# K and V blocks of a decode-attention loop requested as two halves of 64 partitions from two queues

## The chip, the cores and the metric

The kernel runs on one core of one Trainium2 chip. The metric is the device time of one execution in microseconds (us), and the median of several executions is compared. Beside it stands one profiled execution, from which all views of the profile are taken.

## The reference, cut to what matters

One token `x` of 448 values goes through two branches. The first is attention with 16 query heads over 8 groups of a cache of 65,536 keys and values of 256 numbers each (bf16); two query heads share one group. The second is a small token mixer. A sigmoid gate mixes the two.

```python
def _A_ref(x, k_cache, v_cache, wq, wo):
    B, Sq, D = x.shape
    Hq, Dh = 16, 256
    Hkv = k_cache.shape[1]
    rep = Hq // Hkv
    q = (x @ wq).reshape(B, Sq, Hq, Dh).transpose(0, 2, 1, 3)
    k = jnp.repeat(k_cache, rep, axis=1)
    v = jnp.repeat(v_cache, rep, axis=1)
    scores = jnp.einsum("bhqd,bhkd->bhqk", q, k) * (Dh ** -0.5)
    p = _softmax(scores, axis=-1)
    o = jnp.einsum("bhqk,bhkd->bhqd", p, v)
    return o.transpose(0, 2, 1, 3).reshape(B, Sq, Hq * Dh) @ wo
...
return g * a + (1 - g) * b      # g: gate, a: attention, b: mixer
```

K and V together are 8 x 65,536 x 256 x 2 values of 2 bytes, 537 MB. Each of them is used once.

## The kernel before, in words

The cache is cut into 32 blocks of 16,384 positions (`BLK`), four for each group. A block of K or of V is 128 partitions x 128 positions x 256 numbers, so that each partition reads one contiguous row of 65,536 bytes: 8.389 MB in all.

A loop over `t` runs 15 times and does two blocks, `e` = 0 and 1, in four stages. In the first stage of a block VectorE transposes K in eight pieces (`transposes`, L407) and TensorE multiplies each with the queries (`scores`, L415). In the second stage come the softmax (`softmax`, L472 to L511: the maximum, the Exp on ScalarE at L503, the transposed weights), the products with V (`pv`, L435) and the running sum (`accumulate`, L516). The last two blocks are written out behind the loop, with loads cut in other ways (L127, L135, L161); the first K block is requested ahead of it (L132).

K has three buffers of half a block each (`slots`, 64 positions of every partition). A block with `e` = 0 lies in the first two and is transposed upper half first, a block with `e` = 1 lies in the last two, so the next K can be requested when half of the block at hand is transposed. V has one buffer (`vt`), so the next V can be requested when the last product with the block at hand is done.

All large loads are requested by SP, in the order of the program: V of this block (`load_v`, L135), K of the next (`load_k_whole`, L132), and for `e` = 0 a piece of the output weights (`load_wo_wide`, L144), 32 rows of 7,168 bytes that are placed 4 partitions apart. ScalarE requests only the small tables ahead of the loop. In the loop ScalarE does, in this order, two copies of the spread output weights (L564, when TensorE's `spread_wo`, L560, is done), one more copy (L567), the Exp and a small Exp for the rescaling (L507), and again the two Exps for `e` = 1.

`seq` keeps every engine's instructions in the order of the program. The loop's semaphores are reset in turn at the four stages' ends: an engine that enters a stage waits until its own work of two stages before is done, SP's transfers among it (these waits carry the line L602 of the loop).

Of the kernel before, what the change touches and what calls it, by code (L numbers as in the profile page):

```python
# [21 lines left out]
KP = VP // 2  # L22
# [11 lines left out]
def kernel(  # L34
# [15 lines left out]
    nc = tc.nc  # L50
# [12 lines left out]
    def seq(ins):  # L63
        e = ins.ins.engine
        if e in last:
            tc.add_manual_dep(
                ins.ins,
                last[e],
                mybir.DependencyInfo(
                    mybir.DependencyClass.NoSync, mybir.DependencyReason.DATA  # L70
                ),
                reason="program order",
            )
        last[e] = ins.ins.name
        return ins
# [9 lines left out]
    k_all = kvpool.tile([128, 3 * KP, DH], BF16, name="k_all")  # L85
    slots = [k_all[:, i * KP:(i + 1) * KP, :] for i in range(3)]
    vt = kvpool.tile([128, VP, DH], BF16, name="vt")
# [35 lines left out]
    def rows(name, n):  # L123
        return flat[name][bass.ds(n, 1)].rearrange("o p j d -> (o p) j d")
# [6 lines left out]
    def load_k_whole(n, slot):  # L131
        seq(nc.sync.dma_start(out=k_all[:, slot * KP:(slot + 2) * KP, :], in_=rows("k", n)))  # L132

    def load_v(n, j0=0, j1=VP):
        seq(nc.sync.dma_start(out=vt[:, j0:j1, :], in_=rows("v", n)[:, j0:j1, :]))  # L135

    def pairs(ap):
        return ap.rearrange("p (i j) d -> p i j d", i=2)
# [4 lines left out]
    def load_wo_wide(h):  # L143
        seq(nc.sync.dma_start(  # L144
            out=wo_in[0:128:WS],
            in_=A_wo.rearrange("(h q c) n -> h q c n", q=128 // WS, c=WC)[bass.ds(h, 1)].rearrange(
                "o q c n -> (o q) c n"
            ),
        ))
# [9 lines left out]
    def load_v_last(n):  # L159
# [8 lines left out]
        out=wq_t[:, :], in_=A_wq[DM:D, :].rearrange("r (h n) -> (r h) n", h=2)  # L168
    ))
    seq(nc.sync.dma_start(out=wq_m, in_=A_wq[0:DM, :].rearrange("(p k) n -> p k n", k=3)))  # L170
    for k, table in enumerate((
# [19 lines left out]
        out=val[:], in_=rowsel[:, :, :, 0:NI], op=ALU.add, axis=AXIS.XY  # L191
    ))
    fst = const.tile([128, 2, REP], FP32)
    for e in range(2):
        seq(nc.vector.tensor_reduce(
            out=fst[:, e, :], in_=rowsel[:, :, :, e:e + 1], op=ALU.add, axis=AXIS.XY
# [3 lines left out]
        out=par[:], in_=ident_f[:].rearrange("p (a r) -> p r a", r=REP), op=ALU.add, axis=AXIS.X  # L200
# [3 lines left out]
        out=nval[:], in0=val[:], scalar1=-scale, scalar2=None, op0=ALU.mult  # L204
# [7 lines left out]
        out=same[:], in_=val[:].unsqueeze(1).to_broadcast([128, 64, REP])  # L212
# [8 lines left out]
        out=sel[:],  # L221
        in_=ident.rearrange("p (w k) -> p w k", w=NW).unsqueeze(2).to_broadcast([128, NW, NQ, 32]),
# [7 lines left out]
        out=xrr[:], in_=xr[:, DM:D].unsqueeze(2).to_broadcast([1, D - DM, 2])  # L230
    ))
    x_col = hd_ps[:, 40:44]
    for k in range(3):
# [13 lines left out]
        out=xtm[:], in0=par[:], scalar1=x_col[:, 3:4], scalar2=None, op0=ALU.mult  # L247
# [19 lines left out]
        out=veps[:], in0=mv[:, 1:2], scalar1=1e-5, scalar2=None, op0=ALU.add  # L267
# [5 lines left out]
    for _ in range(2):  # L273
# [3 lines left out]
            out=ntmp[:], in0=ntmp[:], scalar1=-0.5, scalar2=1.5, op0=ALU.mult, op1=ALU.add  # L277
# [3 lines left out]
        out=h_bc, in0=xf, scalar1=mv[:, 0:1], scalar2=rstd[:, 0:1],  # L281
        op0=ALU.subtract, op1=ALU.mult,
    ))
    for b in range(NF):
        seq(nc.scalar.activation(
            out=gel[b], in_=h_bc, func=ACT.Gelu_apprx_tanh,
# [33 lines left out]
    for k in range(2):  # L320
        seq(nc.vector.tensor_copy(
            out=qq[:, :, :, k, :], in_=qq_ps.rearrange("p (w g r) -> p w g r", g=HKV, r=REP)
# [72 lines left out]
    def turn():  # L395
        seq(nc.vector.tensor_scalar(
            out=caps[:], in0=caps[:], scalar1=-1.0, scalar2=None, op0=ALU.mult
        ))
        seq(nc.vector.tensor_scalar(
            out=ends[:], in0=ends[:], scalar1=-1.0, scalar2=1.0, op0=ALU.mult, op1=ALU.add  # L400
        ))
# [21 lines left out]
    def score_block(e, pair, hooks={}, order=FORWARD):  # L423
        for k, i in enumerate(order):
            transposes(pair, i)
            scores(e, i, k == 0, k == NI - 1)
            if k in hooks:
                hooks[k]()
# [92 lines left out]
    def denominators():  # L521
        seq(nc.tensor.matmul(  # L522
            hd_ps[:, 460:461], lhsT=same[:].rearrange("p a r -> p (a r)"), rhs=lsum[:, 0:1],
            start=True, stop=True,
        ))
        seq(nc.vector.reciprocal(out=rden[:], in_=hd_ps[:, 460:461]))
        seq(nc.vector.tensor_scalar(
            out=esc[:], in0=fst[:], scalar1=rden[:, 0:1], scalar2=ends[:, 0:1],
            op0=ALU.mult, op1=ALU.mult,
        ))  # L530
# [13 lines left out]
    def head_end():  # L544
        collect(esc, True, True)
        for c in range(2):
            seq(nc.vector.tensor_copy(out=oT[:, c, :], in_=o_ps[c]))  # L547
        a_ps = hd_ps[0:1, 0:D]
        for r in range(REP):
            for c in range(2):  # L550
                seq(nc.tensor.matmul(  # L551
                    a_ps, lhsT=oT[:, c, r:r + 1], rhs=wo_sb[:, r, c, :],
                    start=(r == 0 and c == 0), stop=(r == REP - 1 and c == 1),
                ))
        seq(nc.vector.tensor_tensor(out=a_acc[:], in0=a_acc[:], in1=a_ps, op=ALU.add))  # L555

    def spread_wo(r):
        for c in range(2):
            for u in range(WS):
                seq(nc.tensor.matmul(  # L560
                    wo_ps[c], lhsT=steps[:, WS - u:WS - u + 128], rhs=wo_in[:, 2 * u + c, :],
                    start=(u == 0), stop=(u == WS - 1),
                ))
            seq(nc.scalar.copy(out=wo_sb[:, r, c, :], in_=wo_ps[c]))  # L564

    def older_wo():
        seq(nc.scalar.copy(out=wo_sb[:, 0], in_=wo_sb[:, 1]))  # L567
# [3 lines left out]
    def products(e):  # L571
        for ip in range(NI // 2):
            pv(e, ip)
            if ip == 0:
                tc.previous_stage_wait(mybir.EngineType.PE)
        accumulate(e)
# [19 lines left out]
    def early_signals(i):  # L596
        def both():
            tc.previous_stage_wait(mybir.EngineType.PE)
            tc.previous_stage_wait(mybir.EngineType.DVE)
        return {i: both}  # L600

    with tc.For_i(0, HQ - 1, 1, iteration_sync="staggered") as t:  # L602
        for e in range(2):
            if e:
                tc.stage_boundary()
            if e == 0:
                spread_wo(1)
                head_end()
                older_wo()
            tc.previous_stage_wait(mybir.EngineType.Activation)  # L610
            score_block(
                e, (e, e + 1), early_signals(0), FORWARD if e else UPPER_FIRST
            )
            load_v(2 * t + e)
            tc.stage_boundary()
            if e == 0:
                load_k_whole(2 * t + 1, 1)
                load_wo_wide(t)
                softmax(e, may_begin=True)
                tc.previous_stage_wait(mybir.EngineType.DVE)  # L620
                tc.previous_stage_wait(mybir.EngineType.Activation)
                products(e)
            else:
                load_k_whole(2 * t + 2, 0)
                softmax(e, pair=t + 1)
                tc.previous_stage_wait(mybir.EngineType.DVE)
                tc.previous_stage_wait(mybir.EngineType.Activation)
                denominators()
                turn()
                products(e)  # L630
# [6 lines left out]
    for n in (L - 1, L):  # L637
# [4 lines left out]
        if n == L - 1:  # L642
            load_v(n, 0, 48)
            load_k(L, 0, 2)
            load_k(L, 1, 1)
            load_v(n, 48, VP)
        else:
            load_v_last(L)
            load_wo(HQ - 1, 1)
        if n < L:  # L650
            softmax(n % 2)
        else:
            def rest_base():
# [9 lines left out]
                out=lsv[:], in0=val[:], scalar1=lsum[:, 0:1], scalar2=None, op0=ALU.mult  # L663
# [8 lines left out]
                out=rdv[:], in0=rdv[:], scalar1=gcol[:, 0:1], scalar2=None, op0=ALU.mult  # L672
# [6 lines left out]
    for c in range(2):  # L679
# [9 lines left out]
        out=oT[:], in0=o_last, in1=rdv[:].unsqueeze(1).to_broadcast([128, 2, REP]), op=ALU.mult  # L689
# [43 lines left out]
```

## Time and profile before

| what | value |
|---|---|
| median of 3 runs | 1264.24 us (1263.73 to 1264.41) |
| the profiled execution's own time | 1264.3 us |
| its span, first to last instruction | 1262.5 us |
| mean granted TensorE clock | 0.813 |
| busy: PE, DVE, ACT | 821.7, 711.4, 75.6 us |
| bytes read | 544.22 MB, 431 GB/s over the span |
| K requests in the loop and ahead of it, request to landing | 28.1 us (median) |
| V requests in the loop, request to landing | 27.1 us (median) |

The span lies between the first and the last instruction; what the device time has beyond it (1.8 us) lies around it. Busy time is the time in which an engine executed something. The time from request to landing includes the wait behind transfers that were requested earlier. A queue q1 in the profile is SP's, q10 ScalarE's.

### The profile page before, as it was taken

To read this page: it belongs to the slowest core of one execution; us is meant where nothing else is said; L and a number is where in the kernel's file an instruction comes from. 1 tells how busy PE (TensorE), PEld (TensorE's weight loads), DVE (VectorE), ACT (ScalarE), POOL (GpSimd) and SP (SyncE) were. 2 spreads that over 40 slices of the span, in tenths; PEclk is the share of its full clock that TensorE was granted. 3 is DMA by queue.
4 is the path that set the end of the run, shared out by engine and by line. 5 is a ranking of instruction groups with operands and counts; after the bars stand their busy time and mean duration, and the time that the engine had idled before them with its cause. 6 is when DMAs were issued, how large, how long until landed. Compare 5 with 4: busy or idle time off the path is not lost.

```text
span 1262.5 us, 12356 instructions
## 1 busy us (share of the span) xinstructions
PE 821.7 (65%) x4818; PEld 330.5 (26%) x4818; DVE 711.4 (56%) x755; ACT 75.6 (6%) x163; POOL 4.8 (0%) x9
## 2 busy tenths in 40 slices
PE   4757566575676756677565766658656586665668
PEld 2222222232222222222222322213222132222224
DVE  5665456664556644566444665446654456654575
ACT  4000000000000000000000000000000000000000
POOL 1000000000000000000000000000000000000000
PEclk8887789777888877878778887788877788877979
DMA  9999999999999999999999999999999999999998
GB/s 414 434 435 432 437 432 432 437 434 418 451 434 418 444 420 436 429 438 432 439 432 439 432 432 439 432 439 432 432 439 432 439 432 432 439 432 435 424 435 351
DMA packets 11478, 544.36 MB, mean 431 GB/s; under 512 B 1513, under 2 KB 1644, under 8 KB 2636
## 3 DMA queue, kind: packets, MB, share of 16 engines
q1 hardware_dynamic: 11378, 544.22, 99.6%
q8 instruction: 6, 0.10, 0.0%
q14 instruction: 4, 0.03, 0.0%
q10 hardware_dynamic: 90, 0.01, 0.0%
HBM read 544.22 MB, written 0.00 MB: 431 GB/s over the span
## 4 chain that ended last, share of the span: by engine, by line
DMA 69%; PE 13%; DVE 12%; issue 4%; SPq 0%; ACT 0%; DVEq 0%
DMA k_all<-in_A_k_cache_dram 67%; PE sc L415 12%; DVE kT L407 12%; DMA k_all<-in_A_v_cache_dram 2%; PE pv_last L560 0%; PE f L560 0%; PE hd_ps L551 0%; PE f L694 0%; ACT p_sb L503 0%; SPq L161 0%; DVE rmax L472 0%; SPq L132 0%; PE sm_ps L537 0%; PE hd_ps L537 0%; PE sm_ps L490 0%
## 5 line engine op out<-in xcount | busy, mean ns | idle before, releaser
L415 PE MATMUL sc<-kT,qz 128*128 128x512 bf16 x2048 | 546.5, 417 | 318.6 <-DVE kT L407 318.4
L407 DVE STREAM_TRANSPOSE kT<-k_all 128x2048 f32<-128x2048 f32 x256 | 570.9, 2283 | 207.6 <-DMA k_all<-in_A_k_cache_dram 157.3
L415 PEld LDWEIGHTS <-qz 128*128 128x128 bf16 x2048 | 211.5, 103 | 652.0 <-issue 472.6
L435 PE MATMUL pv_ps<-vt,pT 128*4 128x512 bf16 x1968 | 173.5, 529 | 27.3 <-DVE pT L510 27.3
L516 DVE SCALAR_TENSOR_TENSOR acc<-acc,al,pv_ps 128x512 f32<-128x512 f32 x31 | 23.2, 747 | 161.8 <-PE pv_ps L435 161.8
L435 PEld LDWEIGHTS <-pT 128*4 128x4 bf16 x2000 | 57.2, 109 | 130.8 <-issue 85.9
L503 ACT ACTIVATE p_sb<-sc,nb 128x512 bf16<-128x512 f32 x32 | 22.0, 687 | 1022.7 <-DVE nb L499 1022.7
L472 DVE TENSOR_REDUCE rmax<-sc 128x1 f32<-128x512 f32 x32 | 22.1, 692 | 63.7 <-PE sc L415 63.7
L510 DVE STREAM_TRANSPOSE pT<-p_sb 128x512 bf16<-128x512 bf16 x32 | 22.8, 711 | 27.1 <-ACT p_sb L503 27.1
L522 PE MATMUL hd_ps<-lsum,same 128*128 128x1 f32 x30 | 7.6, 321 | 28.8 <-DVE lsum L511 28.8
L490 PE MATMUL sm_ps<-mrun,ones_f 1*128 1x2 f32 x64 | 12.1, 257 | 21.2 <-DVE mrun L489 12.9
L476 PE MATMUL sm_ps<-ident_f,rmax 128*1 128x128 f32 x32 | 8.7, 270 | 24.5 <-DVE rmax L472 24.5
L560 PE MATMUL pv_last<-wo_in,steps 128*128 128x448 bf16 x64 | 15.6, 369 | 5.1 <-DVEq L602 4.3
L560 PEld LDWEIGHTS <-steps 128*128 128x128 bf16 x128 | 11.6, 100 | 22.2 <-issue 14.0
L490 PEld LDWEIGHTS sm_ps<-mrun,ones_f 1*128 1x128 f32 x64 | 9.4, 183 | 27.4 <-DVE mrun L489 16.3
L555 DVE TENSOR_TENSOR a_acc<-a_acc,hd_ps 1x448 f32<-1x448 f32 x15 | 9.1, 608 | 12.3 <-PE hd_ps L551 12.3
L564 ACT CAST wo_sb<-pv_last 128x448 bf16<-128x448 f32 x16 | 8.5, 532 | 123.7 <-PE pv_last L560 123.7
L551 PE MATMUL hd_ps<-wo_sb,oT 128*1 128x448 bf16 x60 | 15.8, 351 | 0.0
L560 PE MATMUL f<-wo_in,steps 128*128 128x448 bf16 x64 | 15.5, 367 | 0.0
L567 ACT COPY wo_sb<-wo_sb 128x896 bf16<-128x896 bf16 x15 | 14.1, 937 | 14.5 <-PE hd_ps L551 14.5
L522 PEld LDWEIGHTS hd_ps<-lsum,same 128*128 128x128 f32 x30 | 6.3, 261 | 30.1 <-DVE lsum L511 30.1
L547 DVE CAST oT<-hd_ps 128x2 bf16<-128x2 f32 x15 | 2.4, 160 | 20.3 <-PE hd_ps L537 20.3
(124 smaller groups left out, 194.9 us busy)
## 6 DMA issues: line engine op xcount, KB each, us to landing
k_all<-in_A_k_cache_dram SPq DMA_DIRECT2D x2, 4096.0 KB
vt<-in_A_v_cache_dram SPq DMA_DIRECT2D x1, 5120.0 KB
k_all<-in_A_v_cache_dram SPq DMA_DIRECT2D x1, 4096.0 KB
wo_in<-in_A_wo_dram SPq DMA_DIRECT2D x15, 224.0 KB, 27.9
vt<-in_A_wq_dram SPq DMA_DIRECT2D x1, 3072.0 KB
vt<-in_A_v_cache_dram SPq DMA_DIRECT2D x1, 3072.0 KB
k_all<-in_A_v_cache_dram SPq DMA_DIRECT2D x1, 2048.0 KB
k_all<-in_A_v_cache_dram SPq DMA_DIRECT2D x1, 1024.0 KB
```

What stands on the lines that cost most here:

```text
L407: seq(nc.vector.transpose(out=kT_tiles[i % 2][:].rearrange("p j w k c -> p (j w k c)").bitcast(FP32), in_=slots[pair[i // 4]][:, i % 4 * N ...
L415: seq(nc.tensor.matmul(sc_tiles[e][:, :], lhsT=qz[:, 2 * w + c, 2 * (NI - i):2 * (NI - i) + 128], rhs=kT_tiles[i % 2][:, :, w, :, c], star ...
L435: seq(nc.tensor.matmul(dst[32 * grp:32 * grp + 2 * REP, :, :], lhsT=pT[:, 32 * jj + 2 * REP * ip:32 * jj + 2 * REP * (ip + 1)], rhs=pairs( ...
L472: seq(nc.vector.tensor_reduce(out=rmax[:], in_=sc_ps[:, :], op=ALU.max, axis=AXIS.X))
L490: seq(nc.tensor.matmul(sm_ps[:, 128:128 + REP], lhsT=ones_f[0:1, :], rhs=mrun[0:1, :], start=True, stop=True))
L503: seq(nc.scalar.activation(out=p_sb[:, :], in_=sc_ps[:, :], func=ACT.Exp, scale=scale, bias=nb[:, 0:1], accum_out=den[:, 0:1],))
L510: seq(nc.vector.transpose(out=pT[:, :], in_=p_sb[:, :]))
L516: seq(nc.vector.scalar_tensor_tensor(out=acc[:], in0=acc[:], scalar=al_tiles[e][:, 0:1], in1=src[:, :, :], op0=ALU.mult, op1=ALU.add,))
L522: seq(nc.tensor.matmul(hd_ps[:, 460:461], lhsT=same[:].rearrange("p a r -> p (a r)"), rhs=lsum[:, 0:1], start=True, stop=True,))
L551: seq(nc.tensor.matmul(a_ps, lhsT=oT[:, c, r:r + 1], rhs=wo_sb[:, r, c, :], start=(r == 0 and c == 0), stop=(r == REP - 1 and c == 1),))
L560: seq(nc.tensor.matmul(wo_ps[c], lhsT=steps[:, WS - u:WS - u + 128], rhs=wo_in[:, 2 * u + c, :], start=(u == 0), stop=(u == WS - 1),))
L567: seq(nc.scalar.copy(out=wo_sb[:, 0], in_=wo_sb[:, 1]))
```

## The change

`load_k_both` and `load_v_both` request a block in two transfers: partitions 0 to 63 from SP's queue, and partitions 64 to 127 from ScalarE's. Each has 64 rows of 65,536 bytes. They take the place of `load_k_whole` and `load_v` in the loop; ahead of the loop and behind it the loads stay as they were. V's request now stands ahead of the block's scores in the program. On SP the order of the requests is unchanged. On ScalarE the V half of `e` = 0 comes ahead of the copies of L564, the V half of `e` = 1 behind the Exps of `e` = 0, and each K half ahead of the Exp of its block.

```diff
+    halves = ((slice(0, 64), nc.sync), (slice(64, 128), nc.scalar))
+
+    def load_k_both(n, slot):
+        for p, queue in halves:
+            seq(queue.dma_start(
+                out=k_all[p, slot * KP:(slot + 2) * KP, :], in_=rows("k", n)[p]
+            ))
+
+    def load_v_both(n):
+        for p, queue in halves:
+            seq(queue.dma_start(out=vt[p], in_=rows("v", n)[p]))
...
             if e:
                 tc.stage_boundary()
+            load_v_both(2 * t + e)
             if e == 0:
                 spread_wo(1)
                 head_end()
...
             score_block(
                 e, (e, e + 1), early_signals(0), FORWARD if e else UPPER_FIRST
             )
-            load_v(2 * t + e)
             tc.stage_boundary()
             if e == 0:
-                load_k_whole(2 * t + 1, 1)
+                load_k_both(2 * t + 1, 1)
                 load_wo_wide(t)
...
             else:
-                load_k_whole(2 * t + 2, 0)
+                load_k_both(2 * t + 2, 0)
                 softmax(e, pair=t + 1)
```

## The prediction

> **What bounds it now.** I read the page's transfer rows first, then its chain, then one turn of the loop by windows, critical chain, SP's waits and its timeline. The page's rows of the sixteen DMA engines and of their queues:
>
> ```profile
> DMA packets 11478, 544.36 MB, mean 431 GB/s; under 512 B 1513, under 2 KB 1644, under 8 KB 2636
> q1 hardware_dynamic: 11378, 544.22, 99.6%
> q10 hardware_dynamic: 90, 0.01, 0.0%
> ```
>
> Queue q1 is SP's. Its packets fill 99.6% of sixteen engines' span, so about 0.4% (5 us) of the span is free of traffic; the window 1250 to 1262.5 alone, at a DMA share of 0.60, holds all of that. q10 is ScalarE's and carries only the small tables of the start. The chain agrees:
>
> ```profile
> DMA 69%; PE 13%; DVE 12%; issue 4%; SPq 0%; ACT 0%; DVEq 0%
> ```
>
> Its PE and DVE shares are no slack to be won: transfers run under them too, as the windows of whole turns show (the columns end in clock, DMA share and GB/s):
>
> ```profile
> 182.00:260.00 78.00, 49.15 (x284) 19.75 (x282) 43.08 (x45) 3.92 (x9) 0.00 (x0) 0.82 1.00 433
> 260.00:338.00 78.00, 52.31 (x300) 21.52 (x297) 44.18 (x47) 4.99 (x11) 0.00 (x0) 0.82 1.00 433
> ```
>
> One block of K or V is 128 rows of 65,536 bytes, 8.389 MB. In the trace's packet records a row is one packet; each engine takes 8 rows of a block, one behind the other, and 7,486 of 7,808 rows take exactly 2.418 us. So a block takes 8 x 2.418 = 19.34 us, and sixteen engines move 433.7 GB/s, the rate of the windows. A turn has four blocks and 0.55 us of wo_in (two rows of 0.272 us per engine): 77.9 us, against 78.3 between SP's V requests at 102.95 and 181.27. SP's requests come well ahead of their turn:
>
> ```profile
> 181.27 0.34 SPq L135 DMA_DIRECT2D vt<-in_A_v_cache_dram  x1
> 198.61 0.33 SPq L132 DMA_DIRECT2D k_all<-in_A_k_cache_dram  x1
> 199.19 0.49 SPq L144 DMA_DIRECT2D wo_in<-in_A_wo_dram  x1
> 216.73 0.34 SPq L135 DMA_DIRECT2D vt<-in_A_v_cache_dram  x1
> ```
>
> K landed at 187.9 and 226.7 (the critical chain), so V has the engines from 187.9 to 187.9 + 19.34 = 207.2. The K request of 198.61 comes 8.6 us before that end, the V request of 216.73 10 us before 226.7. What times a request is a buffer coming free, and a stage's end:
>
> ```profile
> SPq L602 <- DMA vt<-in_A_v_cache_dram: 243.8, 30, 9.2
> SPq L132 <- DVE kT L407: 238.4, 30, 8.5
> SPq L135 <- PE pv_ps L435: 153.4, 29, 6.2
> ```
>
> None of these waits shows as an idle DMA engine. The bound is the rate of the rows, 2.418 us each.
>
> **The change, part by part.** The loop runs 15 times; 60 requests of 8.389 MB become 120 of 4.194 MB, half of them on ScalarE. Everything before and behind the loop stays.
>
> Issue on ScalarE: 60 x 0.34 us (SP's row) = 20 us of its sequencer, at nothing. The K half waits for the transposes of its stage; behind it stands the Exp L503, which waits for VectorE's nb in any case (1022.7 us over 32), and at 211.41 it started 12.8 us after SP's K request. The V half waits for the last P.V product (its end about 181.2); behind it stands the cast L564, which at 182.04 waited for TensorE's spread_wo, so 0.34 us plus the start of an issue just fits between. Were the cast 0.3 us late, K's landing at 187.9 would still cover it; without cover it is 15 x 0.3 = 4.5 us, at most 20. load_v moves ahead of score_block in the text, but SP runs nothing of score_block and its V request keeps the same waits: nothing.
>
> SP's stage waits now take in both halves' landings: at equal rates of the two rings, nothing. Bytes are the same. End marks: 16 more packets of 9 ns per block, one per engine, 60 x 0.009 = 0.5 us, and 0.5 us is below what a measurement of this kernel can tell from no change (about 0.2%, 2.5 us).
>
> What is left, and is everything, is how the engines run the rows. Two facts bear on it. First, an engine that has packets in both rings takes one from each in turn: in the packet records, from 4.4 us on, one 256-byte packet of q10 stands between two 24,576-byte rows of q1, on engine after engine, and none runs beside another. Second, a request of 64 rows puts 4 on each engine, as 128 rows put 8 and wo_in's 32 rows put 2. Both halves are asked for within a microsecond, so all sixteen engines write a row of partitions 0 to 63, then all a row of 64 to 127.
>
> No row of this trace shows sixteen engines inside one half of the partitions, so the cost is bounded. Upper end: a row load of 128 partitions has one engine on each eighth-row group of 8 partitions at 27.1 GB/s (65,536 / 2.418), and no row shows a group of 8 taking more. With twice the engines per group in the half being written, each row takes 4.836 us, a block 38.7, and 60 blocks cost 60 x 19.34 = 1160.6 us more. Lower end: wo_in has 32 rows only, and each still ran at its full rate, 7,168 bytes in 0.272 us, so the engine alone may be the limit and the cost nil; but its rows lie 4 partitions apart over all 128, and are a ninth as long. Below nothing: size against time (7,168 in 0.272, 65,536 in 2.418) leaves 8.4 ns of fixed time per row, and if a second ring hid that, 60 x 8 x 0.0084 = 4.0 us would be gained. I take a value near the upper end: the wide 128-row loads are the nearest in length, and in them each part of the partitions gets 1/16 of the rate and never more. The full factor 2 needs all engines in step. Around 66 us of the span their rows start within 1.37 us, thirteen of sixteen within 0.44 us; a mean pair is some 0.4 us apart, 17% of a row, in which each has its half to itself; a block lands with its last pair, which is nearly in step. I take the middle, 10% saved: 0.9 x 1160.6 = 1045 us.
>
> [...]
>
> Sum on the profiled execution: its time is 1264.3 us (span 1262.5 and 1.8 around it), 0.06 above the median of 1264.24. 1264.2 + 1045 = 2309 us. The last loads (L127, L135, L161) keep 128 rows and their 19.34 us per block.
>
> What is late next: K's landing, as now. With 38 us per transfer the requests (10.7 us behind a landing) come far ahead of the engines, so no wait on SP or ScalarE matters.
>
> **Rivals.**
>
> Out of step: the engines slide apart, so that one writes the lower half while its partner writes the upper. For: with the sixteen starts spread over 1.37 of 2.418 us, a pair at the two ends is 57% out of step already, and single rows of up to 2.97 us push engines about. Against: in the loop an engine that runs ahead waits for the next request, and all start it together. At 57% for all pairs the cost is 0.43 x 1160.6 = 499 us, 1763 in all; the case runs from 1320 to 1900.
>
> No shared limit (not slower): the engine itself is the limit and partitions take what comes. For: 7,486 rows at one time to the nanosecond, and wo_in's 27 GB/s in 32 rows. Against: only its rows' spread. It decides if a row of a half still takes 2.418 us. Then the same rows run in another order and the two halves of a block land together: 0 to +1.5 us, 1264 to 1266. It is also the case in which the change does nothing, or in which the hardware deals rows by partition, so that one half is eight engines' work. [...]
>
> Rings out of phase: rows stay at 2.418 us, but wo_in's two packets per engine sit in SP's ring alone, so ScalarE's ring gets ahead by up to two rows, and V's lower half lands behind rows of the next K. V is needed at 212.98 (P.V starts) and landed about 207.2: 5.7 us, 2.4 rows of cover. If a third row comes between, P.V and then the next V request slip; at 2.4 us per turn that is 15 x 2.4 = 36 us, 1300; the case runs from 1267 to 1320.
>
> Faster: the 8.4 ns per row hidden by the other ring, 1264.2 - 4.0 = 1260.2. It needs an engine that begins a row of one ring before the other's ends; against it, the q10 packets of the start stand one behind the other. The loop has no other time to give.
>
> **How the numbers follow.** In step, near factor 2: 0.55. Out of step: 0.18. No shared limit: 0.16. Rings out of phase: 0.06. Faster: 0.05. Slower by over 0.2%: 0.55 + 0.18 + 0.06 = 0.79; within 0.2%: 0.16; faster: 0.05. The predicted time is that of the first case, 2309, whose own range is 1900 to 2430 (55% of the upper end: 1264 + 638 = 1902; the whole of it and 5 us of late casts and marks: 1264 + 1161 + 5 = 2430). For 8 in 10 the range must hold the first two cases and reach to a third; the one at 1264 is the next, so it runs from 1262 to 2430.
>
> **What would show it.** Right: q1 and q10 with about half the bytes each (some 290 and 252 MB); DMA share still near 1.00 but about 225 to 245 GB/s in the loop's windows; K's requests landing after some 60 to 75 us instead of 28; VectorE's wait L407 for k_all up from 157.3 us by about a thousand; the sixteen engines' rows at 4 to 5 us. No shared limit: 433 GB/s, split evenly, rows at 2.418 us. Rings out of phase: rows at 2.418 us, but windows with a share under 1.00, and TensorE's L435 waiting for vt. Casts in the way: L564 starting behind an issue of ScalarE, and the next wo_sb product late. The prediction is wrong in its one large term if a row of a half does not take about twice as long.

## The result and the profile after

The changed kernel takes 2492.22 us (2487.4 to 2496.72, 4 runs) against 1264.16: a ratio of 1.9715 (95% interval 1.9677 to 1.9753). Here and below, runs that lie more than 1.5% above the fastest of their kernel are slow executions, and comparisons leave them out. The profiled execution took 2487.4 us, with a span of 2485.4. Lines of the loop's body stand 12 further down than before (the transposes are L419, the scores L427, P.V is L447, the loop L614).

The page of the changed kernel, its transfer rows:

```profile
DMA packets 12438, 544.36 MB, mean 219 GB/s; under 512 B 2474, under 2 KB 2605, under 8 KB 3597
q1 hardware_dynamic: 7538, 292.56, 52.2%
q10 hardware_dynamic: 4890, 251.67, 47.7%
```

The bytes are those of before. The two queues hold what the change puts on them, and together they fill 99.9% of the engines' span. So the engines are not idle: they are slow, at 219 GB/s against 431 before. The loop's windows say by how much (the last three columns are clock, DMA share and GB/s):

```profile
200.00:356.00 156.00, 50.19 (x284) 20.29 (x284) 43.64 (x44) 3.92 (x9) 0.00 (x0) 0.65 0.99 210
356.00:512.00 156.00, 50.09 (x284) 20.05 (x284) 43.51 (x44) 3.92 (x9) 0.00 (x0) 0.66 1.00 210
```

A turn that did 433 GB/s does 210, at the same share. TensorE's work per turn is the same (50 us), at a lower granted clock, 0.65 against 0.82; it waits for data either way. Who waits now, of the groups of waits (us in total, times, longest):

```profile
DVE kT L419 <- DMA k_all<-in_A_k_cache_dram: 934.7, 31, 33.9
PE pv_ps L447 <- DMA vt<-in_A_v_cache_dram: 473.2, 30, 25.3
```

VectorE's wait for K was 157.3 us. TensorE's wait for V is new. And SP's own waits and the requests' times to landing (in the page's part on DMA issues, the last number is the median in us):

```profile
SPq L614 <- DMA k_all<-in_A_k_cache_dram: 963.6, 29, 34.2
SPq L614 <- DMA vt<-in_A_v_cache_dram: 842.2, 30, 33.9
SPq L141 <- DVE kT L419: 119.6, 17, 8.4
```

```profile
k_all<-in_A_k_cache_dram SPq DMA_DIRECT2D x31, 65.5
vt<-in_A_v_cache_dram ACTq DMA_DIRECT2D x30, 46.1
vt<-in_A_v_cache_dram SPq DMA_DIRECT2D x30, 73.6
k_all<-in_A_k_cache_dram ACTq DMA_DIRECT2D x30, 47.1
```

SP's requests of V land 27 us behind ScalarE's, and V is complete only with the slower half. No run shows why. My guess is that wo_in's packets are in SP's ring alone (a ring is here what one engine runs of one queue's packets), so that ScalarE's ring runs ahead. The packet records of the trace give the size of the loss. They name no engine, but a packet that begins where another ends can be put on the same engine. Of 7,808 rows of 65,536 bytes 126 took about 2.42 us (the first block, which is still whole). Of the others, 5,050 took between 4.75 and 5 us (mean 4.879) and 2,623 more than 5 us (mean 5.087).

### The profile page after: what moved, and what is told of

Its sections match the earlier page's. It is cut to its first block, busy times and chain, and to the rows that moved or that the text cites. A ratio compares the mean times of both kernels' runs of the same rounds, so it can differ in the third digit from the quotient of the medians.

```text
span 2485.4 us, 12694 instructions
## 1 busy us (share of the span) xinstructions
PE 819.3 (33%) x4818; PEld 331.0 (13%) x4818; DVE 711.4 (29%) x755; ACT 75.6 (3%) x163; POOL 4.8 (0%) x9
## 3 DMA queue, kind: packets, MB, share of 16 engines
q1 hardware_dynamic: 7538, 292.56, 52.2%
q10 hardware_dynamic: 4890, 251.67, 47.7%
## 5 line engine op out<-in xcount | busy, mean ns | idle before, releaser
L427 PE MATMUL sc<-kT,qz 128*128 128x512 bf16 x2048 | 543.5, 415 | 1096.9 <-DVE kT L419 1096.6
L419 DVE STREAM_TRANSPOSE kT<-k_all 128x2048 f32<-128x2048 f32 x256 | 570.8, 2283 | 983.0 <-DMA k_all<-in_A_k_cache_dram 934.7
L427 PEld LDWEIGHTS <-qz 128*128 128x128 bf16 x2048 | 210.7, 103 | 1428.1 <-issue 1247.0
L447 PE MATMUL pv_ps<-vt,pT 128*4 128x512 bf16 x1968 | 173.6, 529 | 473.2 <-DMA vt<-in_A_v_cache_dram 473.2
L447 PEld LDWEIGHTS <-pT 128*4 128x4 bf16 x2000 | 59.0, 109 | 576.2 <-issue 532.7
L502 PEld LDWEIGHTS sm_ps<-mrun,ones_f 1*128 1x128 f32 x64 | 9.4, 182 | 27.4 <-DVE mrun L501 16.3
L341 DVE COPY qz<-qq 32x16 bf16 (+1 forms) x64 | 10.5, 163 | 1.4
```

Source lines behind the costliest of these rows:

```text
L419: seq(nc.vector.transpose(out=kT_tiles[i % 2][:].rearrange("p j w k c -> p (j w k c)").bitcast(FP32), in_=slots[pair[i // 4]][:, i % 4 * N ...
L427: seq(nc.tensor.matmul(sc_tiles[e][:, :], lhsT=qz[:, 2 * w + c, 2 * (NI - i):2 * (NI - i) + 128], rhs=kT_tiles[i % 2][:, :, w, :, c], star ...
L447: seq(nc.tensor.matmul(dst[32 * grp:32 * grp + 2 * REP, :, :], lhsT=pT[:, 32 * jj + 2 * REP * ip:32 * jj + 2 * REP * (ip + 1)], rhs=pairs( ...
L502: seq(nc.tensor.matmul(sm_ps[:, 128:128 + REP], lhsT=ones_f[0:1, :], rhs=mrun[0:1, :], start=True, stop=True))
```

## The experiments

Three theories were set against each other first. "Half": all engines write into one half of the partitions at a time, and a half takes no more than half of the rate. "Turns": an engine that changes queue after every row loses time. "Reads": the rows of the cache that are read together collide.

**One queue.** The same halves, both from SP.

```diff
-    halves = ((slice(0, 64), nc.sync), (slice(64, 128), nc.scalar))
+    halves = ((slice(0, 64), nc.sync), (slice(64, 128), nc.sync))
```

> The same halves of 64 neighbouring partitions, both requested from SP's queue, the lower one first. Theory 'half' (all sixteen engines write into one half of the partitions at a time, and a half takes only half of the rate): rows stay near 4.85 to 4.95 us, 2430 to 2500 us in all. Rival 'turns' (an engine that changes queue after every row loses a row's time): rows back at 2.42 us, 1264 to 1270. Rival 'reads' (the rows of the cache that are read together collide): the same rows are read together, 2430 to 2500.

2544.79 us, a ratio of 2.0149 (2.0109 to 2.0189). "Turns" falls: with one queue the loss is larger, not gone. The page:

```profile
DMA packets 12438, 544.37 MB, mean 215 GB/s; under 512 B 2473, under 2 KB 2604, under 8 KB 3596
q1 hardware_dynamic: 12338, 544.22, 99.9%
```

In its packet records the pattern is regular. Each engine has four rows of one half and then four of the other; a row that follows a row of the same half takes 5.12 to 5.14 us, and the first row after a change of half mostly 4.82 to 4.94. The two queues of the change switch halves at most rows: of the 7,651 rows that can be joined to the row before them on their engine, 4,871 follow a row of the other half and take 4.88 us on average, the other 2,780 take 5.07. So most of its rows are of the cheaper kind. The shorter rows are what it gains over one queue, 53 us.

**Every second partition.** Two queues, 64 rows per request from neighbouring rows of the cache, but they land in the even and the odd partitions.

```diff
-    halves = ((slice(0, 64), nc.sync), (slice(64, 128), nc.scalar))
+    halves = ((slice(0, 128, 2), slice(0, 64), nc.sync), (slice(1, 128, 2), slice(64, 128), nc.scalar))
...
-                out=k_all[p, slot * KP:(slot + 2) * KP, :], in_=rows("k", n)[p]
+                out=k_all[p, slot * KP:(slot + 2) * KP, :], in_=rows("k", n)[r]
...
-            seq(queue.dma_start(out=vt[p], in_=rows("v", n)[p]))
+            seq(queue.dma_start(out=vt[p], in_=rows("v", n)[r]))
```

> Two queues and 64 rows a request as in the change, and the same rows of the cache in each request, but they land in every second partition (even ones from SP, odd ones from ScalarE), so that each request covers the whole width. In blocks 0 and 30 keys then meet the values of other positions, since one of the two is loaded elsewhere; the work is the same. 'half': 1264 to 1275 us, rows of 2.42 us. 'turns': about 2490. 'reads': about 2490.

1355.09 us, a ratio of 1.0718 (1.07 to 1.0736). The rows are back: 7,364 of 7,808 take 2.42 to 2.6 us. Number of rows, queues and rows read are those of the change; only the partitions differ, and they take away 1137 of 1228 us. Of the 91 us that are left, 71 are engines without work. The queues fill all but 76 us of this kernel's span, and all but 5 of before's:

```profile
q1 hardware_dynamic: 7538, 292.56, 51.5%
q10 hardware_dynamic: 4890, 251.67, 42.9%
```

The other 20 us are in slower rows (up to 3.7 us); most of these are the first that an engine runs after a time without work. SP's waits and a window of a loop's stretch:

```profile
SPq L141 <- DVE kT L419: 458.7, 30, 17.3
```

```profile
200.00:356.00 156.00, 95.44 (x512) 37.38 (x515) 85.25 (x84) 5.85 (x15) 0.00 (x0) 0.78 0.94 400
```

The K request waits for all eight transposes of the block, not for four: with the transposes of K beginning at 662.9 it goes out at 682.16, 19.2 us later, where before it was 10.6. With 8.6 us of lead gone the engines run dry (share 0.94). That this wait takes in transposes of the other buffer is how the program's waits came out for strided partitions, no property of the chip.

**Every second row.** The halves of the change, but each reads every second row of the cache.

```diff
-    halves = ((slice(0, 64), nc.sync), (slice(64, 128), nc.scalar))
+    halves = ((slice(0, 64), slice(0, 128, 2), nc.sync), (slice(64, 128), slice(1, 128, 2), nc.scalar))
```

> The halves of the partitions as in the change, two queues, but each request reads every second row of the cache (even rows to the lower half, odd rows to the upper). In blocks 0 and 30 keys meet the values of other positions, as before. 'half': as the change, 2430 to 2500 us. 'turns': about 2490. 'reads': well below, near 1264 if the neighbouring rows were the whole cause.

2498.05 us, a ratio of 1.9785 (1.9728 to 1.9842): the interval overlaps that of the change. "Reads" falls.

**K on SP, V on ScalarE, both whole.**

```diff
     def load_k_both(n, slot):
...
+        load_k_whole(n, slot)
...
     def load_v_both(n):
...
+        seq(nc.scalar.dma_start(out=vt[:], in_=rows("v", n)))
```

> Whole blocks of 128 partitions, K from SP's queue and V from ScalarE's, V's request where the change has it. 'half': 1264 us within 3 (each engine has its own partitions). 'turns': the two queues hold rows together for some 9 us of every 19 us block, so 1700 to 1900 us. 'reads': 1264. It also prices the moved V request and its place on ScalarE: nothing expected.

1274.54 us, a ratio of 1.0077 (1.0054 to 1.01). Two queues and the moved V request together cost some 10 us. "Half" expected at most 3: a small effect is missing from it. The guess was that ScalarE's rows of V get in between K's last rows and so make K late. The next two runs test that.

**V alone, every second partition, from two queues and from one.** K is whole on SP. The comments name the two runs.

```diff
+    halves = ((slice(0, 128, 2), nc.sync), (slice(1, 128, 2), nc.scalar))   # v_every_second
+    halves = ((slice(0, 128, 2), nc.sync), (slice(1, 128, 2), nc.sync))     # v_every_second_one_queue
...
     def load_k_both(n, slot):
...
+        load_k_whole(n, slot)
...
             seq(queue.dma_start(out=vt[p], in_=rows("v", n)[p]))
```

> V in two requests of 64 rows from two queues, even partitions from SP and odd ones from ScalarE, each from its own row of the cache; K whole on SP, requested after four transposes again. 'half': rows of 2.42 us, 1264 to 1276 us (ScalarE's rows of V may pass the last rows of K as in the run with K and V on two queues, which took 1274.5). If the 91 us that every second partition cost for K and V together came of the requests themselves and not of K's later request, about 1310.

> V in two requests of 64 rows, even and odd partitions, but both on SP's queue behind K. If the 11 us that the same rows cost from two queues came of ScalarE's rows of V passing the last rows of K, they are gone: 1264 to 1266 us. If they came of two requests in place of one, or of V's place in the program: 1275 us.

From two queues 1275.39 us (ratio 1.0089, 1.007 to 1.0108), from one 1264.38 (ratio 1.0001, 0.9992 to 1.001). So splitting a block in two requests and asking for V earlier in the text cost nothing here, and the second queue costs 11 us. VectorE's wait for K, first from two queues and then from one:

```profile
DVE kT L416 <- DMA k_all<-in_A_k_cache_dram: 179.8, 22, 16.3
```

```profile
DVE kT L416 <- DMA k_all<-in_A_k_cache_dram: 155.2, 30, 7.7
```

With one queue the longest wait for K is 7.7 us, with two 16.3. The reading that fits is that V's rows in a ring of their own run between K's, which were asked for first, and K is what the next block waits for. That rows of two queues mix on an engine, the changed kernel's records show (4,871 of 7,651 follow one of the other queue). The 80 us between 1355 and 1275 go with K's halves, whose late request is described above; no run shows that alone.

**V alone in the halves of the change.** K is whole on SP, `halves` as in the change.

```diff
     def load_k_both(n, slot):
-        for p, queue in halves:
...
+        load_k_whole(n, slot)
```

> Only V comes in the two halves, K stays whole on SP. If each half row costs by itself ('half'), half of the loss is left: 1264 + 1228 / 2 = 1878 us, in a range of 1850 to 1910. If the loss came of K and V halves standing in the way of each other, much less than half is left: below 1700.

2002 us (2001.73 and 2002.29; two further executions took 2055.63 and 2062.38): a miss for "half" as stated, since 738 of 1228 us are left, not 614. The rows account for 693 us of it. Rows of V's half that follow one another take 5.13 us. Where the two rings alternate, V's take 4.5 to 4.95, and K's whole-width rows between them 2.6 to 3.0 in place of 2.42. A row of V and the K row behind it together take some 7.5 us, as 5.13 and 2.42 do. So it reads as if a row of V handed part of its cost to the next row. Some 33 us more are engines without work: the queues fill all but 38 us of this kernel's span, and all but 5 of before's.

```profile
q1 hardware_dynamic: 9458, 418.39, 68.6%
q10 hardware_dynamic: 2490, 125.84, 29.5%
```

The last 11 us or so are in smaller packets that took longer; wo_in's, at 0.45 us against 0.27, are about half of it.

**Where the border lies.** Two kernels move the cut by 32 partitions, one from two queues and one from SP alone; a third cuts in four. The comments name the first two.

```diff
+    halves = ((slice(32, 96), nc.sync), (slice(0, 32), nc.scalar), (slice(96, 128), nc.scalar))  # middle
+    halves = ((slice(32, 96), nc.sync), (slice(0, 32), nc.sync), (slice(96, 128), nc.sync))      # middle_one_queue
+    halves = tuple((slice(32 * i, 32 * (i + 1)), (nc.sync, nc.scalar)[i % 2]) for i in range(4)) # quarters
```

> Four requests of 32 partitions per block, 0 to 31 and 64 to 95 from SP, 32 to 63 and 96 to 127 from ScalarE, so that the engines are on partitions 0 to 63 first and then on 64 to 127. 'Fold': 32 neighbouring partitions are as good as 64, rows of 4.85 to 5.15 us, 2470 to 2560 us. 'Width' (the rate goes with the number of partitions written at a time): rows of about 9.7 us, 1264 + 3 x 1161 = 4750 us.

2513.14 us, a ratio of 1.9873 (1.984 to 1.9906), against 2492.22 with 64 neighbouring partitions and the 4750 of "width". 32 neighbouring partitions do within 1% as well as 64: "width" falls.

> SP requests partitions 32 to 95, ScalarE 0 to 31 and 96 to 127. 'Fold' (0 to 31 and 32 to 63 are one receiving half, 64 to 127 the other, so 32 to 95 reaches both): SP's rows 2.42 us when alone, ScalarE's 4.85 to 5.12, so 60 x 4 x 2.5 = 600 us over before, about 1860 (1700 to 2000). 'Neighbours' (any 64 neighbouring partitions take half of the rate): all rows near 4.9, about 2490.

The four executions of this kernel were far apart, 2500.8 to 2568.9 us, and the profiled one is the longest. By its time "neighbours" would stand. But the rows of the profiled execution took anything from 2.4 to 7.8 us, with two kinds of request mixed on each engine. It decides nothing, and the one-queue form was made to separate them.

> All on SP's queue: partitions 32 to 95 first, then 0 to 31, then 96 to 127, so that all engines are in one request at a time and its rows can be read by themselves. 'Fold': rows of 32 to 95 take 2.42 us, the others 5.12, about 1264 + 60 x 4 x 2.7 = 1912 us. 'Neighbours' (any 64 neighbouring partitions, or 32, take half of the rate): all rows near 5.12, about 2545 us.

2312.23 us, a ratio of 1.8288 (1.8253 to 1.8323). The time misses both expectations, but the rows can be read. In the block that begins at 701 us, fourteen of sixteen engines run three successive rows of partitions 32 to 95 in about 2.42 us each (the last of them, on two engines, in 2.55 and 2.88), and then, without a gap, rows of 0 to 31 and 96 to 127 that mostly take 4.8 to 5.4. So these 64 neighbouring partitions, which lie on both sides of partition 64, are no trouble at 2.42 us, where rows of 0 to 63 mostly took 4.75 to 5.14 in the runs above: of the two theories "fold" fits and "neighbours" falls.

The same records show two things more. First, a row inside one half is not slow by itself: of the rows of 0 to 31 and 96 to 127 that can be told by their order, 21 ran while on average fewer than three other engines wrote, and 20 of them took 2.42 us. Second, rows that run at the same time are not slowed alike. In the block at 701 us one engine is ahead and already in 0 to 31, and one is late in 32 to 95: their rows, side by side from 704 us on, take 4.47 and 4.46 us while the fourteen take 2.42. From 1137 us on at most six engines write, and from 1139.5 on only four: three of these take 6.85 to 7.05 us for a row, nearly three times 2.42, and the fourth takes 2.42. It reads as if the engines shared something narrower than a half. What that is, and which partitions it takes in, no run shows.

The time is also long because the engines ran dry. The queue fills all but 279 us of the span (the first row has tenths in 40 slices):

```profile
DMA  9999988979798788978898888979798897988877
q1 hardware_dynamic: 13298, 544.23, 87.9%
```

## Why the prediction was wrong, point by point

The cause was right, as far as the runs show it: rows take about twice as long when a request lies inside one half of the partitions (a mean of 4.949 us against 2.418). The one large term was too small. The forecast was 2309 us with an upper end of 2430; it came out at 2492.

The bound (the engines' rows), the bytes on each queue (some 290 and 252 MB predicted, 292.56 and 251.67 found) and K's landing (60 to 75 us predicted, 65.5 found on SP) came as predicted. At the turn looked at, the issue on ScalarE was free, with the margin named. Its timeline there:

```profile
332.20 0.52 ACTq L147 DMA_DIRECT2D vt<-in_A_v_cache_dram  x1
332.97 0.53 ACT L576 CAST wo_sb<-pv_last 128x448 bf16<-128x448 f32 x1 [26.42 <-PE pv_last L572]
```

The issue took 0.52 us, not the 0.34 of SP's row, and still ended before the cast, which waited for TensorE as before.

The step that failed is the term for the rows: "0.9 x 1160.6 = 1045 us". The rows cost 7,682 x (4.949 - 2.418) / 16 = 1215 us, of a difference between the two profiled executions of 2487.4 - 1264.3 = 1223 us. The term was 170 us short, in two ways.

First, the 10% saved for engines out of step (116 us) does not exist. The engines did slide apart. At 45 us of the span eight write into one half and eight into the other, and all sixteen rows take 4.86 to 4.91 us. In 27 rows of the loop an engine had its half to itself, with all fifteen others in the other half, as in the row that begins at 709.48 us; these rows took 5.09 to 5.11. An engine out of step gained nothing. Why not is open: with few engines at work, a row in one half took 2.42 us (the run with 32 to 95 from one queue), so it is not the row by itself. Whether engines that write elsewhere hold it up, or its own row before, no run separates.

Second, the "upper end" was no upper end (the other 55 us). It let a half take exactly half of the full rate, 4.836 us per row, by counting the engines on each group of 8 partitions; that count was my estimate, since the records name neither engine nor partition. In steady writing to one half a row takes 5.12 (the run with one queue), which is 16 x 65,536 / 5.12 = 205 GB/s and not 217. Halves in turn soften that to 4.88, the same half twice in a row does not (5.07 in the changed kernel), and the mean of 4.949 lies above my ceiling. With the measured row the sum is 1264 + 1215 = 2479 us, half a percent under the result.

Of the rivals, "no shared limit" is refuted by the rows, which would have stayed at 2.418 us. A second queue was not free either: in the pair of V runs it cost 11 us (1275.39 against 1264.38).

"Rings out of phase" occurred as a delay, whatever its cause. It shows in V's halves landing 27 us apart and in TensorE's 473.2 us for V, where I had named K alone as late; but since the engines are full to 99.9% it shifts the waiting and adds little of its own. wo_in's rows, the evidence against the limit, were explained rightly as spread over both halves: the even and odd partitions ran at 2.42 us too. "Out of step" came true as a movement and was worth nothing, as shown above. "Faster" did not occur.

VectorE's wait for K rose by 777 us, not by about a thousand, while TensorE's new wait for V took 473.2 us. The windows did 210 GB/s where 225 to 245 were expected, which is the mis-sized row again.

## What to carry to other kernels

Here the DMA engines were full for the whole span (99.6%), and a split of the same bytes gained nothing and lost 1228 us. In such a profile ask which partitions each request covers, not how many requests or queues there are: every second partition in place of the two halves took away 1137 of the 1228 us, one queue in place of two none. If a load must be cut, the cut that cost nothing here had each part on both sides of partition 64 (V in every second partition on one queue, 1264.38 us); from a second queue the same cut cost 11 us, so keep what is needed first ahead on the same queue. A bound made from "no row shows more" is a guess about the ceiling: half of a measured rate is not the least that half of the resource can give.

## What the runs showed of the hardware that was not expected

- Rows that follow one another in one half took 5.12 us (both halves from one queue): 205 GB/s for sixteen engines, less than half of the 433 before.
- The cost of a row seems to be paid partly by the next one: the first row after a change of half took 4.82 to 4.94 us (both halves from one queue), and whole-width rows after half rows 2.6 to 3.0 in place of 2.42 (V alone in halves).
- In the changed kernel an engine that has a half to itself is held up all the same, at 5.09 to 5.11 us per row (27 rows).
- Rows that run at the same time are not slowed alike: with four to six engines at work, three took 6.85 to 7.05 us per row and another 2.42 (32 to 95, one queue).
- The granted clock was 0.813 before and 0.663 after, with nearly the same busy time on TensorE (821.7 and 819.3 us) in a span of 1262.5 and 2485.4 us.
